# First feed-forward product of tiles 4 to 15 by one Strassen level, in blocks of 512 tokens

## The chip, the core and the metric

The kernel runs on one core of a Trainium2 chip. Its engines work side by side and meet at semaphores: TensorE (PE: matmuls out of SBUF into PSUM), VectorE (DVE), ScalarE (ACT), GpSimd (POOL) and SyncE (SP), and the DMA queues that SyncE and ScalarE feed. The metric is the device time of one launch in microseconds, lower is better. Before the change it is 388.39 us, the median of three runs (388.04 to 388.52).

## The reference

One transformer block on 2048 tokens of width 576, in bf16. Only its shape matters here:

```
h = layernorm(x) * (1 + ca) + sa
x = x + ga * attention(h)        # 32 heads of 18, linear attention, then @ wo
h = layernorm(x) * (1 + cb) + sb
x = x + gb * (relu(h @ w1) @ w2) # w1: 576 x 4608, w2: 4608 x 576
```

`attention` makes features phi(q), phi(k) of width 36 a head, sums kv over all tokens, and gives each token phi(q) kv / (phi(q) z).

## The kernel before

The 2048 tokens are 16 tiles of 128. A first part, whose order is written out word by word in `ORDER`, does the norms, the k, v and q projections of all tiles, the sums kv, the attention of tiles 0 and 1, and the loads of the weights. Its last feature tiles of q go to HBM (`eqd`) and come back later.

The second part is a loop over 8 blocks of 256 tokens (two tiles). A block has two stages, and its program order is the order of the Python calls: each engine runs its own instructions in that order.

- `l1` is the first feed-forward product. The hidden width is 36 chunks of 128, taken as 18 pairs (one of each half). The input width 576 is 4 chunks of 128 and one of 64. `l1_full` (L673) does the chunks of 128 with 256-column matmuls; `l1_rest` (L680) does the chunks of 64, two at a time in the upper and lower half of the rows. The work is in three groups of three PSUM pairs. `relu` (L687 to L689) takes the two halves of the hidden chunks and tokens out of PSUM as A11, A12, A22 and the difference U3; L711 makes the sum U2.
- `l2` is the second product, by one Strassen level: 7 products of 18 matmuls of 288 columns (L735) in place of 8. Its weight sums T1 to T4 are made once, in block 0, by `t_part`, and all weights stay in SBUF (R1, R2, RT). X, Y and Z are the three PSUM banks of its sums. `fin` (L718 to L722) scales a result, adds the residual row in `x_sb` and leaves it to a store.

Into both stages go "hooks" for the next block: `attend` (scores L389, reciprocal and scaling L396 and L397, a DMA transpose), the output projection (`wo_rest` L807 and `wo_full` L813), the residual add (L411) and statistics (L238), `norm2` (L420, a DMA transpose), the scale and shift of the norm (L851), and `q_next` (sums L282, reciprocal L341, GpSimd's L344 and L289, a DMA transpose L348, a reload L337). The scores and the projection share one PSUM pair, `pair(3)`.

## Time and profile before

The profiled execution has a span of 386.3 us, from the first to the last instruction; the median of the runs is 388.39.

| what | from the profile |
|---|---|
| TensorE, matmuls | 379.6 us busy, 98% of the span, 3705 matmuls |
| VectorE, ScalarE, GpSimd | 63%, 41%, 32% |
| granted TensorE clock | 1.000 |
| DMA | 43.18 MB, mean 112 GB/s |
| first 90 us | the part in `ORDER` |
| one block of 256 tokens (blocks 1 to 4) | 36.71 us, TensorE busy for all of it |
| last block | from 348.44 us to the end, 37.86 us |

A line of the page's groups reads: line, engine, operation, output<-inputs, shape (partitions x elements, type), count | busy us, mean ns of one | idle us just before, and what ended the idle time. The chain that ended last follows the work back from the last instruction; in order of time each line has its start, its length and what ran.

### The profile page before, as it was taken

What the parts mean: (1) busy time and instruction counts of PE and PEld (TensorE: products, weight loads), DVE (VectorE), ACT (ScalarE), POOL (GpSimd) and SP (SyncE); (2) the same over time, 40 slices, a digit from 0 to 9 for tenths busy, and PEclk for the clock granted to TensorE, in tenths of its full rate; (3) what the DMA queues carried; (4) which work ended last, traced back from release to release, by engine and by line L of the source; (5) the groups of instructions that cost most, each with busy time, mean ns of one, the idle gap of its engine ahead of it and who ended that gap; (6) DMA issues with size and microseconds to landing.
All of it is one profiled execution on the core that took longest, in us unless ns stands there. A gap on an engine that the chain in (4) does not pass through costs nothing.

```text
span 386.3 us, 8923 instructions
## 1 busy us (share of the span) xinstructions
PE 379.6 (98%) x3705; PEld 309.7 (80%) x3705; DVE 242.6 (63%) x470; ACT 156.7 (41%) x380; POOL 125.3 (32%) x195
## 2 busy tenths in 40 slices
PE   7999999999999999999999999999999999999995
PEld 4887778888887887788888888887888788778874
DVE  2898998784898666744764584567456735542333
ACT  2689997688540233034303420451054023302510
POOL 2088889830106400620160035004500540041023
PEclk9999999999999999999999999999999999999999
DMA  7995799798510524241233024212631221200001
GB/s 301 420 417 209 261 394 360 137 259 277 84 34 19 75 53 51 47 110 34 50 76 82 20 49 110 48 19 52 122 36 20 46 63 36 36 0 32 3 0 34
DMA packets 48940, 43.18 MB, mean 112 GB/s; under 512 B 39297, under 2 KB 41986, under 8 KB 48130
## 3 DMA queue, kind: packets, MB, share of 16 engines
q1 hardware_dynamic: 48610, 42.41, 39.4%
q8 instruction: 29, 0.48, 0.5%
q10 hardware_dynamic: 288, 0.19, 0.2%
q14 instruction: 13, 0.11, 0.1%
HBM read 27.38 MB, written 5.90 MB: 86 GB/s over the span
## 4 chain that ended last, share of the span: by engine, by line
PE 87%; DMA 4%; ACT 4%; DVE 3%; issue 1%; POOL 1%; SPq 0%; POOLq 0%; DVEq 0%
PE PS L673 33%; PE PS L735 31%; PE PS L272 9%; PE PS L680 5%; PE PS L813 4%; ACT RT L277 3%; DMA x_sb<-in_xk_dram 2%; PE PS L389 2%; DMA R<-in_wkT_dram 2%; PE PS L322 1%; DVE Rk L282 1%; PE PS L406 1%; DVE st L238 1%; ACT RT L511 0%; PE PS L807 0%
## 5 line engine op out<-in xcount | busy, mean ns | idle before, releaser
L673 PE MATMUL PS<-h,R 128*128 128x256 bf16 x1152 | 132.1, 273 | 0.0
L673 PEld LDWEIGHTS <-R 128*128 128x128 bf16 x1152 | 111.4, 98 | 14.1 <-issue 0.6
L735 PEld LDWEIGHTS <-RH 128*128 128x128 f16 x846 | 82.7, 98 | 20.7
L721 POOL TENSOR_TENSOR yt<-yt,gb_row 128x288 f32<-128x288 f32 x23 | 28.0, 1219 | 202.7 <-DVE yt L720 202.7
L687 ACT ACTIVATE RH<-PS 128x256 f16<-128x256 f32 x72 | 27.5, 382 | 110.6 <-PE PS L680 92.3
L735 PE MATMUL PS<-R,RH 128*128 128x288 bf16 (+1 forms) x558 | 72.1, 286 | 0.0
L689 DVE SCALAR_TENSOR_TENSOR RH<-PS,RH 128x256 f16<-128x256 f32 x72 | 28.6, 412 | 61.0 <-ACT RH L687 61.0
L688 ACT ACTIVATE RH<-PS 128x512 f16<-128x512 f32 x72 | 42.9, 596 | 5.5 <-PE PS L673 4.6
L277 ACT ACTIVATE RT<-PS,rs 128x576 bf16<-128x576 f32 x64 | 42.8, 742 | 2.3 <-PE PS L272 1.8
L735 PE MATMUL PS<-RT,RH 128*128 128x288 f16 x288 | 37.9, 286 | 0.0
L739 ACT ACTIVATE RS<-PS 128x288 f32<-128x288 f32 x24 | 9.8, 410 | 65.2 <-PE PS L735 65.2
L272 PE MATMUL PS<-RH,R 116*128 116x288 bf16 x240 | 32.5, 286 | 0.1
L272 PE MATMUL PS<-RH,RT 116*128 116x288 bf16 x240 | 31.9, 286 | 0.3
L720 DVE TENSOR_TENSOR yt<-PS,RS 128x288 f32<-128x288 f32 x23 | 10.5, 455 | 31.0 <-PE PS L735 21.9
L238 DVE BATCH_NORM_STATS2 st<-x_sb 128x6 f32<-128x288 bf16 x64 | 25.9, 447 | 4.0 <-DMA x_sb<-in_xk_dram 3.4
L272 PEld LDWEIGHTS <-RT 116*128 116x128 bf16 x240 | 22.9, 98 | 6.0 <-issue 0.5
L272 PEld LDWEIGHTS <-R 116*128 116x128 bf16 x240 | 22.7, 98 | 6.0 <-issue 0.5
L722 POOL TENSOR_TENSOR x_sb<-yt,x_sb 128x288 bf16<-128x288 f32 x31 | 22.7, 731 | 2.9 <-DVE yt L718 1.1
L282 DVE TENSOR_REDUCE Rk<-RT 128x64 f32<-128x1152 bf16 x16 | 21.3, 1336 | 0.9 <-ACT RT L277 0.7
L282 DVE TENSOR_REDUCE Rq<-RT 128x64 f32<-128x1152 bf16 x16 | 21.5, 1343 | 0.0
L680 PE MATMUL PS<-h,R 64*128 64x256 bf16 x288 | 19.9, 271 | 0.0
L411 DVE TENSOR_TENSOR x_sb<-x_sb,PS 128x576 bf16<-128x576 bf16 x16 | 12.1, 754 | 11.3 <-PE PS L813 10.2
(119 smaller groups left out, 418.8 us busy)
## 6 DMA issues: line engine op xcount, KB each, us to landing
R<-in_w1a_dram SPq DMA_DIRECT2D x4, 1152.0 KB, 8.2
eqd<-RT SPq DMA_DIRECT2D x12, 288.0 KB, 2.1
RT<-eqd SPq DMA_DIRECT2D x12, 288.0 KB, 3.5
R<-in_w2b_dram SPq DMA_DIRECT2D x2, 1296.0 KB, 8.1
R<-in_w2a_dram SPq DMA_DIRECT2D x3, 864.0 KB
out_dram<-x_sb SPq DMA_DIRECT2D x15, 144.0 KB, 2.1
RT<-in_xT_dram SPq DMA_DIRECT2D x2, 640.0 KB, 14.0
x_sb<-in_xk_dram SPq DMA_DIRECT2D x3, 288.0 KB
```

The costliest lines, as they stand in the source:

```text
L238: dve.bn_stats(out=s[:, hf, :], in_=x_sb[:, t, hf * HD:(hf + 1) * HD])
L272: pe.matmul(pr[:, k, 0:HD], lhsT=xt(t, ck), rhs=w[0:R, ck, k * HD:(k + 1) * HD], start=(ck == 0), stop=(ck == NC - 1))
L277: act.activation(out=E.rearrange("p (b h s e) -> p b h s e", b=2, s=2, e=DH)[:, :, :, s, :], in_=pr[:, :, 0:HD].rearrange("p b (h e) -> p ...
L282: dve.tensor_reduce(out=Rr, in_=E.rearrange("p (c e) -> p c e", e=DH), axis=AXX, op=ALU.add)
L673: pe.matmul(PS[:, 2 * u + hf, n * 256:n * 256 + 256], lhsT=w1a[:, ci, jj * P:(jj + 1) * P], rhs=hb[:, ci, :], start=(n == 0 and ci == 0), ...
L680: pe.matmul(PS[:, 2 * u + hf, n * 256:n * 256 + 256], lhsT=w1b[b0:b0 + 64, j * P:(j + 1) * P], rhs=hb[b0:b0 + 64, 4, :], start=False, stop ...
L687: act.activation(out=A11[:, j, :], in_=lo[:, :, 0, :], func=ACT.Relu)
L688: act.activation(out=A2[:, j, :, :], in_=PS[:, 2 * u + 1, :].rearrange("p (n s f) -> p n s f", n=2, s=2), func=ACT.Relu)
L689: dve.scalar_tensor_tensor(out=U3[:, j, :], in0=lo[:, :, 1, :], scalar=0.0, in1=A11[:, j, :], op0=ALU.max, op1=ALU.subtract)
L721: pool.tensor_tensor(out=y, in0=y, in1=gb_row[:, c], op=ALU.mult)
L722: pool.tensor_tensor(out=x_sb[:, t, c], in0=y, in1=x_sb[:, t, c], op=ALU.add)
L735: pe.matmul(PS[:, bank, 0:HD], lhsT=am[:, j, :], rhs=bm[:, j, :], start=first and j == 0, stop=(j % 9 == 8), skip_group_check=True)
```

## The change

Tiles 0 to 3 (two blocks of 256) go as before. Tiles 4 to 15 go in three blocks c of 512 tokens, with new stages.

- `c_l1` is the first product of 512 tokens by one Strassen level over tokens x input (the chunks of 128) x hidden. Each of 9 groups makes two pairs of hidden chunks by 7 products of 4 matmuls (L928), where 8 products of 4 stood. Four of the seven use sums of the weights, f16, three of them in three rotating slots (`ring`) in the upper half of `x_sb`, and one in place of w1 itself; four use sums of the activations, S1 to S4 (`h_sums`). Partial sums stay in PSUM: ScalarE copies a bank into another and one into SBUF (L959, L961), VectorE adds that to a bank, into PSUM (L981, L998), and further matmuls go on adding there. Four matmuls with zeros a block (`set_bits`) touch the upper columns of four banks. The chunks of 64 stay as they were, in one run a group (`ham`).
- The weight sums are made in blocks 0 and 1 by `sums1`, go to HBM (`w1td`, `sums1_out`), and come back piece by piece (`ring_in`). `x_sb` holds eight tiles then, and the rows of later tiles are loaded again.
- `c_l2` is the second product for 512 tokens: the same seven products, each for the two halves p of 256 columns. Its weights are seven quarters a block, read from HBM into four slots (`quarter_in`, ScalarE's queue); T1 to T4 are written to HBM once (`sums2_out`).
- The hooks of a block of 512 cover four tiles: the sums of q in `c_l1`, the scores, projection and norms in `c_l2`. Tiles 6 to 15 use the projection with ten full matmuls (`wo_mm`). The subtraction A12 - U2 goes from VectorE to GpSimd, in three parts.

```diff
--- before.py
+++ after.py
+NG = NK // 2
...
+    w2td = dram.tile([4, P, TW], FP16, name="w2td")
+    w1td = dram.tile([P, NG, 6 * 2 * P], FP16, name="w1td")
...
-    oT = small([P, 2, NC, P], BF16, "oT")
+    oT2 = [small([P, 2, NC, P], BF16, "oT"), carve(me, 0, (2, NC, P))]
+
+    def oT(t):
+        return oT2[t // 2 % 2][:, t % 2]
+
...
-    w2 = [carve(R2[i], 0, (NK, D)) for i in range(2)]
+    SLOTS = [R2[0][:, 0:TW], R2[1][:, 0:TW], R2[0][:, TW:], R2[1][:, TW:]]
+    B11, B21, B12, B22 = (v.rearrange("p (a b) -> p a b", b=HD) for v in SLOTS)
+    T3 = carve(R2[0].bitcast(FP16), TW, (NK, HD))
+    RTh = RT.bitcast(FP16)
+    T1, T4, T2 = (carve(RTh, i * TW, (NK, HD)) for i in range(3))
...
-        if b > 0:
-            dve.tensor_tensor(out=A12, in0=A12, in1=U2, op=ALU.subtract)
+        for k in range(3):
+            v, u = (x[:, 6 * k:6 * k + 6, :] for x in (A12, U2))
+            pool.tensor_tensor(out=v, in0=v, in1=u, op=ALU.subtract)
...
+    def attend(t, pr, double):
+        num_mm(t, pr)
+        num_o(t, pr)
+        if double:
+            act.activation(out=o_sb[:, t % 2, D:640], in_=o_sb[:, t % 2, 512:D], func=ACT.Copy)
+        turn_dma(oT(t), o_sb[:, t % 2, :])
...
+    ring = x_sb[:, 8:16, :].rearrange("p a b -> p (a b)").bitcast(FP16).rearrange(
+        "p (s m c f) -> p s m c f", s=3, m=3, c=2)
...
+    def sums1(k, s):
+        t1, t2, t4 = (ring[:, s, m] for m in range(3))
+        w12, w11, w22, w21 = (wq_slots(*i, k)[:, s] for i in ((0, 1), (0, 0), (1, 1), (1, 0)))
+        for o, p, q in ((t1, w12, w11), (t2, w22, t1), (t4, w21, t2)):
+            dve.tensor_tensor(out=o, in0=p, in1=q, op=ALU.subtract)
+
+
+    def sums1_out(k):
+        act.dma_start(w1td[:, 3 * k:3 * k + 3, :], ring.rearrange("p s m c f -> p s (m c f)"))
+
...
+    def ring_in(n):
+        g = n % NG
+        act.dma_start(ring[:, g % 3].rearrange("p m c f -> p (m c f)"), w1td[:, g, :])
+
+    QUART = (("in", 0), ("in", 2), ("t", 1), ("t", 0), ("t", 2), ("t", 3), ("in", 3))
+
+    def quarter(n):
+        kind, i = QUART[n % 7]
+        v = SLOTS[n % 4]
+        return (v if kind == "in" else v.bitcast(FP16)).rearrange("p (a b) -> p a b", b=HD)
...
+    def quarter_in(n):
+        kind, i = QUART[n % 7]
+        v = SLOTS[n % 4]
+        if kind == "in":
+            act.dma_start(v, w2in[:, i, :])
+        else:
+            act.dma_start(v.bitcast(FP16), w2td[i])
+
+    def sums2_out(i):
+        act.dma_start(w2td[i], flat((T1, T2, T3, T4)[i]))
...
+    def h_scale(k):
+        c = slice(2 * P * k, 2 * P * (k + 1))
+        for ci in range(NC):
+            act.activation(out=hc[:, ci, c], in_=hc[:, ci, c], func=ACT.Identity, scale=mod2[:, 1, ci:ci + 1],
+                           bias=mod2[:, 0, ci:ci + 1])
+
+    def h_sums():
+        a11, a12, a21, a22 = (hc[:, 2 * f:2 * f + 2, 2 * P * t:2 * P * (t + 1)] for t in range(2) for f in range(2))
+        for o, p, q, op in ((S1, a21, a22, ALU.add), (S2, S1, a11, ALU.subtract), (S3, a11, a21, ALU.subtract),
+                            (S4, a12, S2, ALU.subtract)):
+            dve.tensor_tensor(out=o, in0=p, in1=q, op=op)
+
+    def set_bits(bank):
+        pe.matmul(PS[:, bank, HD:512], lhsT=zero[:, 0:P], rhs=zero[:, 0:512 - HD], start=False, stop=True,
+                  skip_group_check=True)
+
+    def c_l1(c, mid, hooks, tail):
+
+        def xb(g):
+            return PS[:, 2 * (g % 2), :]
+
+        def yb(g):
+            return PS[:, 1 + 2 * (g % 2), :]
+
+        def zb(g):
+            return PS[:, 6 - 2 * (g % 2), :]
+        qb, rb = PS[:, 5, :], PS[:, 7, :]
...
+        def first(g):
+            mm(xb(g), raw(w1a, 0, 0, g), A11, g, True)
+            act.activation(out=yb(g), in_=xb(g), func=ACT.Copy)
+            mm(qb, tw(0, g), S1, g, True)
+            act.activation(out=dd[:, g % 2, :], in_=qb, func=ACT.Copy)
...
+        def group(g):
+            cur, prev, q = g < NG, g > 0, g - 1
+            if cur and prev:
+                first(g)
+            if prev:
+                act.activation(out=js(cA11, q), in_=yb(q), func=ACT.Relu)
+                mm(zb(q), raw(w1a, 1, 1, q), S4, q, False)
+                if not cur:
+                    tail(0)
+                mm(xb(q), tw(2, q), A22, q, False)
+            if g == 0:
+                set_bits(6)
+            if cur:
+                mm(xb(g), tw(1, g), S2, g, False)
+                dve.tensor_tensor(out=zb(g), in0=xb(g), in1=dd[:, g % 2, :], op=ALU.add)
+            top = (rest(yb(g), g, 0, True) if cur else []) + (rest(xb(q), q, 1, True) if prev else [])
+            low = (rest(zb(q), q, 0, False) + rest(rb, q, 1, False)) if prev else []
+            ham(top, low)
+            if prev:
+                dve.scalar_tensor_tensor(out=js(cU3, q), in0=xb(q), scalar=0.0, in1=js(cA11, q), op0=ALU.max,
+                                         op1=ALU.subtract)
+                act.activation(out=js(cA22, q), in_=rb, func=ACT.Relu)
+                act.activation(out=js(cA12, q), in_=zb(q), func=ACT.Relu)
+            if cur:
+                mm(yb(g), raw(w1a, 1, 0, g), A12, g, False)
+                if g == 0:
+                    set_bits(7)
+                mm(xb(g), raw(w1h, 0, 1, g), S3, g, False)
+                if g == 0:
+                    set_bits(3)
+                    set_bits(4)
+                dve.tensor_tensor(out=rb, in0=xb(g), in1=dd[:, g % 2, :], op=ALU.add)
+            mid(g)
+            if prev:
+                pool.tensor_tensor(out=js(cU2, q), in0=js(cU3, q), in1=js(cA22, q), op=ALU.add)
+                n = NG * c + q + 3
+                if n < NG * NCB:
+                    ring_in(n)
+            hooks(g)
...
+        def prod(i, p, lo, hi):
+            banks, am = ((XB, cA11), (YB, cA12), (XB, cU2), (ZB, cA11), (XB, cU3), (XB, cA22), (ZB, cA12))[i]
+            first = i in (0, 3)
+            bm = quarter(7 * c + i)
+            for j in range(lo, hi):
+                if j % 9 == 0:
+                    hooks(done[0])
+                    done[0] += 1
+                    if done[0] == 28 and ahead:
+                        ahead()
+                pe.matmul(PS[:, banks[p], 0:HD], lhsT=am[:, j, p * P:(p + 1) * P], rhs=bm[:, j, :],
+                          start=first and j == 0, stop=(j % 9 == 8), skip_group_check=True)
...
+        def body():
+            prod(0, 0, 9, NK)
+            for i in range(7):
+                for p in range(2):
...
+                        prod(i, p, 0, NK)
+                    ta, tb = t0 + p, t0 + 2 + p
+                    if i == 0:
+                        act.activation(out=PS[:, YB[p], 0:HD], in_=PS[:, XB[p], 0:HD], func=ACT.Copy)
+                    if i == 1:
+                        fin(ta, 0, YB[p], None)
+                        dve.tensor_tensor(out=cols(cA11, p), in0=cols(cU2, p), in1=cols(cA11, p), op=ALU.add)
+                        for k in range(3):
+                            v, u = (cols(x, p)[:, 6 * k:6 * k + 6, :] for x in (cA12, cU2))
+                            pool.tensor_tensor(out=v, in0=v, in1=u, op=ALU.subtract)
+                    if i == 2:
+                        copy(p, 1)
+                    if i == 4:
...
+                    if i == 5:
+                        fin(tb, 0, XB[p], None)
...
+                    if i == 6:
+                        fin(ta, 1, ZB[p], CS[p][1])
+                        store(ta)
+                    if p == 0 and i and 7 * c + i + 3 < 7 * NCB:
+                        quarter_in(7 * c + i + 3)
+            if not last:
+                quarter_in(7 * c + 10)
...
+            q_next(5)
+            sums2_out(1)
+        if pos == 9:
+            q_next(6)
+        if pos == 10:
+            sums2_out(2)
+        if pos == 11:
+            hb = h2[:, 1]
+            for ci in range(NC):
+                dve.tensor_scalar(out=hb[:, ci, :], in0=hb[:, ci, :], scalar1=mod2[:, 1, ci:ci + 1],
+                                  scalar2=mod2[:, 0, ci:ci + 1], op0=ALU.mult, op1=ALU.add)
+        if pos > 10:
+            sums1(2, pos - 11)
...
+        if g and u == 1:
+            pool.memset(o_sb[:, g - 1, D:640], 0.0)
+            attend(5 + g, LOW, False)
+        if (g, u) == (1, 1):
+            q_next(NT)
+        if (g, u) in ((1, 0), (1, 1), (1, 2)):
+            sums1(1, u)
+        if (g, u) == (2, 0):
+            sums1_out(1)
...
+    def b1_l2(pos):
+        if pos == 0:
+            norm2(4, quad(4))
+            norm2(5, quad(5))
+        if pos in (2, 5):
+            t = 6 + pos // 5
+            wo_mm(t, LOW)
+            residual(t, LOW)
+        if pos in (4, 7):
+            t = 6 + pos // 7
+            norm2(t, quad(t))
+        if pos in (1, 3, 4):
+            sums1(0, (1, 3, 4).index(pos))
+        if pos == 6:
+            sums1_out(0)
+        if pos == 8:
+            sums1_in_place(0)
+        if pos in (9, 11):
+            h_scale(pos // 11)
+        if pos == 12:
+            h_sums()
+            quarter_in(2)
...
+        def mid_l1(g):
+            if more and g in (2, 4, 6, 8):
+                q_tail(t + g // 2 - 1)
...
+        def in_l1(g):
+            if c == 0 and g in (0, 2):
+                sums1_in_place(1 + g // 2)
...
+            if g == 2:
+                s = t % 8
+                act.dma_start(x_sb[:, s:s + 4, :], a["xk"][:, t * D:(t + 4) * D].rearrange("p (t d) -> p t d", d=D))
+            if g in (1, 3, 5, 7):
+                q_head(t + g // 2)
...
+            i = {2: 0, 4: 1, 6: 2, 8: 3}.get(pos)
+            if i is not None:
+                attend(t + i, ATT, False)
+            i = {9: 0, 11: 1, 13: 2, 15: 3}.get(pos)
+            if i is not None:
+                wo_mm(t + i, ATT)
+                residual(t + i, ATT)
+            i = {11: 0, 13: 1, 15: 2, 17: 3}.get(pos)
+            if i is not None:
+                norm2(t + i, quad(t + i))
+            if pos in (19, 23):
+                h_scale(pos == 23)
+            if pos == 25:
+                h_sums()
...
+    l1(0, b0_l1)
+    l2(0, b0_l2)
+    l1(1, b1_l1)
+    l2(1, b1_l2, heads[0])
+    quarter_in(3)
+    for c in range(NCB):
+        tail, body = c_l2(c, l2s[c][1], heads[c + 1] if c + 1 < NCB else None)
+        tails = [tail]
+        bodies[c]()
+        body()
```

## The prediction

> **What bounds the kernel now.** I read the page's first part, then the chain that ended last (its shares, then in order of time), then the timeline around the matmul mode changes, then the groups by shape, and last the lines of GpSimd's products.
>
> The page: TensorE is busy nearly the whole span, and the chain is mostly TensorE, two thirds of it in the two feed-forward products (L673 and L735).
>
> ```profile
> PE 379.6 (98%) x3705; PEld 309.7 (80%) x3705; DVE 242.6 (63%) x470; ACT 156.7 (41%) x380; POOL 125.3 (32%) x195
> PE 87%; DMA 4%; ACT 4%; DVE 3%; issue 1%; POOL 1%; SPq 0%; POOLq 0%; DVEq 0%
> ```
>
> One pair of tiles on the chain (columns: start, length, what). All pieces are TensorE's and join up, so this stage has no wait to win; only fewer or shorter matmuls help. A 256-column matmul takes 5.24/48 = 0.1092 us, a 288-column one 15.43/126 = 0.1225.
>
> ```profile
> 201.59 3.06 PE PS L673 x28
> 204.64 0.76 PE PS L680 x12
> 205.40 0.48 PE PS L389 x10
> ...
> 211.50 0.76 PE PS L680 x12
> 212.38 1.09 PE PS L813 x8
> 213.47 5.24 PE PS L673 x48
> ...
> 222.87 15.43 PE PS L735 x126
> ```
>
> The timeline prices a change between full and half-row matmuls. The 48 full ones are issued from 139.88 to 145.12, and the half-row run starts at 145.22: 0.10 us lost. Its six pairs go out at about 0.109 (to 145.87), and the full ones after the last pair (0.122 from 145.88) start at 146.10: 0.10 again, so 0.19 a run with rounding. The last line gives a hand-over: eight matmuls end at 140.04 by the model (issue ends at 139.88), VectorE starts at 140.08, 0.20 after issue.
>
> ```profile
> 138.89 1.15 PE L813 MATMUL PS<-wo_sb,oT 128*128 128x288 bf16 x8
> 139.88 5.40 PE L673 MATMUL PS<-h,R 128*128 128x256 bf16 x48
> ...
> 145.22 0.83 PE L680 MATMUL PS<-h,R 64*128 64x256 bf16 x12
> ...
> 145.88 0.29 PE L807 MATMUL PS<-wo_sb,oT 64*128 64x288 bf16 x2
> 146.10 1.15 PE L813 MATMUL PS<-wo_sb,oT 128*128 128x288 bf16 x8
> ...
> 140.08 0.76 DVE L411 TENSOR_TENSOR x_sb<-x_sb,PS 128x576 bf16<-128x576 bf16 x1 [0.81 <-PE PS L813]
> ```
>
> Durations for the new work (mean ns after the comma):
>
> ```profile
> L688 ACT ACTIVATE RH<-PS 128x512 f16<-128x512 f32 x72 | 42.9, 596 | 5.5 <-PE PS L673 4.6
> L689 DVE SCALAR_TENSOR_TENSOR RH<-PS,RH 128x256 f16<-128x256 f32 x72 | 28.6, 412 | 61.0 <-ACT RH L687 61.0
> L743 DVE TENSOR_TENSOR RH<-RT,RH 128x2304 f16<-128x2304 f16 x8 | 10.9, 1358 | 3.8 <-PE PS L735 3.8
> L720 DVE TENSOR_TENSOR yt<-PS,RS 128x288 f32<-128x288 f32 x23 | 10.5, 455 | 31.0 <-PE PS L735 21.9 <-POOL x_sb L722 9.1
> ```
>
> GpSimd and VectorE get in each other's way: the same product takes 0.73 us or 4.68 (min/median/max), and VectorE's subtraction 1.05 or 1.90.
>
> ```profile
> L721 POOL TENSOR_TENSOR yt<-yt,gb_row x23: 728/730/4682, 119.1 to 378.5; 128x288 f32<-128x288 f32 x23
> L465 DVE TENSOR_TENSOR RT<-R,RT x6: 1048/1050/1900, 102.5 to 120.9; 128x1728 f16<-128x1728 bf16 x6
> ```
>
> **The change, part by part.** The sum is against the profiled execution, span 386.3; the median of 388.39 is 2.1 more, and I carry that over. A measurement tells about 0.2% (0.8 us) from no change.
>
> *TensorE's issue.* (a) Per 512 tokens the first product has 28 matmuls in each of 9 groups, 252, where 288 stood: 108 fewer in three blocks, 108 x 0.1092 = -11.8. (b) Half-row matmuls, equal in number, stood in 3 runs per 256 tokens, 6 per 512; now one per group and one after, 10. Four more runs at 0.19, and the first and last run each lack partners for two (one slot more each, 0.11): +0.98 a block, +2.9. (c) Four zero matmuls of 224 columns a block, 12 x 0.096: +1.15. (d) The output projection of tiles 6 to 15 is ten full matmuls (1.225) in place of a pair and eight (1.10): +1.2. The second product keeps its count, and f16 runs like bf16 in its rows (286 ns both). Sum: -6.5. All of it is on the path.
>
> *The group loop.* Per group TensorE issues 28 x 0.1092 + 4 x 0.109 + 0.19 = 3.69. ScalarE has five 512-wide passes at about 0.65 from start to start (0.60 and a gap): 3.25, hidden. VectorE has two adds into PSUM and one relu-subtract; no row writes PSUM, so from L720's 455 at 288 and a slope near 1.04 ns per element I take 0.69 each, 0.56 start to start. The tight chain: S2's matmuls end, 0.20, add, relu-subtract, next group's first matmul into the bank just read: 0.20 + 0.56 + 0.69 + 0.05 = 1.50. TensorE needs for the work between 0.63 + 2 x 0.437 = 1.50. No slack, so any excess is paid 27 times. I take 0.6 in all; bounds 0 and 0.2 a group (5).
>
> *Streaming.* A quarter of the second weights (1296 KB) is issued 2.5 products (11 us) ahead; the same size landed in 8.1 us before, amid other loads. The first product's sums come in 384 KB pieces with about 4.2 us from issue to use; 288 KB landed in 2.7 to 3.7. I take nothing: what hides them is those products and a group. If that cover is gone, see the third rival. ScalarE issues them in its own order, behind work already released, so nothing queues long.
>
> *Attention inside the second product (blocks of tiles 4 and 8).* Here I see a new wait. One PSUM pair serves the scores of four tiles and then the projection. After product 1's first half VectorE has the final multiply (0.46), the 2304-wide add (1.36), then reciprocal and scaling (0.35 + 0.76) of the third tile: done 3.0 us after that half. The fourth tile's scores are wanted at 0.39 + 18 x 0.1225 = 2.6: 0.4 lost. The second half repeats it: VectorE is done 2.8 later, while the projection is wanted 0.39 + 9 x 0.1225 = 1.5 after those scores start: 1.2 lost. That makes 1.6 a block as the floor. GpSimd now runs three 768-wide subtractions (about 1.48 each, an estimate from 1166 ns at 576 and 2322 at 1280), and if the second add waits behind one it adds 0.85 (1.90 less 1.05): ceiling 2.5. Of the adds beside GpSimd most keep their time (L465's median), some do not; I take 2.0, twice: +4.0. The first scores of each such block wait about 0.3 for two relus of the last group: +0.6.
>
> [...]
>
> *Tiles 0 to 3.* VectorE gets 27 subtractions of 512 for the first weights' sums (0.42 each, from 554 at 768; three in a chain 1.25). End of block 0: three chains and one more attention sum, while the subtraction that went to GpSimd (needed by the last product) competes with them: 0 to 2.5, I take 1.2. Block 1, first product: between the projection of tile 4 and the third relu stand 0.2 + 0.76 + 1.0 + 1.25 + 0.3 + 1.11 + 1.25 + 0.42 = 6.3 of VectorE, and TensorE wants that bank after 0.87 + 0.39 + 1.31 + 2.62 = 5.2: 1.1. Block 1, second product: VectorE starts 1.5 late with 10.7 before tile 7's second norm; logarithm, scaling, transpose (2.6 to 4.1), four passes of 0.49 and the sum follow: 18.2 to 19.7, wanted at 13 x 1.10 + 2.45 + 0.44 = 17.2: 1.0 to 2.5, I take 1.8. Together +4.1, bounds 0.5 and 7.
>
> *The end.* Half-width products, two short VectorE steps and a 2 us store, as before: 0.
>
> Sum: -6.5 + 0.6 + 4.0 + 0.6 + 4.1 = +2.8: span 389.1, time 391.2.
>
> **The rivals.**
> 1. *The saving stays (faster).* If VectorE's backlog in tiles 0 to 3 fits in TensorE's own slack and only the attention floor is paid, waits are 3.2 + 0.6, and the time is 388.4 - 6.5 + 3.8 = 385.7. For it: VectorE had 63% only, idle near 125 us. It decides when all waits stay under 6.5.
> 2. *VectorE bounds the group loop (slower).* If writing PSUM costs 0.1 us more per add than my 0.69, the chain grows by 0.1 to 0.2 in 27 groups, 2.7 to 5.4 on top: 394 to 397, at 0.25 it is 400. For it: no slack; against: the slopes of all PSUM readers agree.
> 3. *A 384 KB piece comes late.* At 3.7 plus a third it needs 4.9, 0.7 over; in the eight groups with attention transfers that is 5.6, in all 27 it is 19: 397 to 410. Against it: 2.7 when quiet, which gives 3.6.
> 4. *The matmuls are not fewer or not faster.* Only if mixed f16 and bf16 ran slower; both stand at 286 ns in L735. Nothing for it.
>
> [...]
>
> **How the numbers follow.** Forecast (waits 7.3 to 13, 389.2 to 395): 0.49. Rival 1: 0.23, all faster. Between them, within 0.2%: 0.05. Rival 2: 0.15. Rival 3: 0.07. Others, slower: 0.01. So faster 0.23, same 0.05, slower 0.72. The range takes rival 1 down to 384 and rivals 2 and 3 up to 400; the forecast's own is 389.2 to 395.
>
> **What would show it.** Right: 1044 full first-product matmuls, no idle between them beyond 0.1 us a group; gaps of 0.4 and over 1 us on TensorE at the fourth scores and first projection of two blocks, released by VectorE; a gap before the first S1 product. Wrong: group periods well over 3.7 us, gaps released by a DMA, or no gaps at those places.

## The result, and the profile after

The changed kernel takes 424.96 us (median of four runs, 423.2 to 425.4) against 388.22 for the kernel before: a ratio of 1.094, 95% interval 1.092 to 1.096. The profiled execution has a span of 423.4 us (before: 386.3). Slower was forecast; 36.7 us slower was not, the forecast was 391.2 and its range ended at 400.

The page of the changed kernel: TensorE's busy share, the clock that it was granted in 40 slices of the span, and the engines' shares of the chain that ended last.

```profile
PE 385.6 (91%) x3607; PEld 303.5 (72%) x3609; DVE 269.1 (64%) x483; ACT 193.5 (46%) x427; POOL 189.9 (45%) x242
...
PEclk9999999999999899999999996899989986999999
...
PE 63%; DVE 14%; DMA 13%; ACT 6%; issue 2%; SPq 1%; ACTq 0%; DVEq 0%
```

TensorE's share of the chain fell from 87% to 63%; VectorE (3% before) and the transfers (4% before) took its place. And around TensorE's long waits the granted clock falls, to 0.6 in one slice, which the page of before does not show.

In the line numbers of the changed kernel, L928 is the first product of tiles 4 to 15, L1025 their second product, L399 the scores, L416 the output projection, L411 the DMA transposes (`turn_dma`), L900 and L907 the scaling and the sums of the transposed rows (`h_scale`, `h_sums`), L867 the ring pieces, L880 and L882 the quarters, L751 the second product of tiles 0 to 3. The groups of instructions, costliest first (busy us, mean ns; then the idle time before them and what ended it):

```profile
L928 PE MATMUL PS<-RT,x_sb 128*128 128x256 f16 x216 | 34.1, 283 | 19.4 <-DVE RT L907 19.4
...
L981 DVE TENSOR_TENSOR PS<-PS,RT 128x512 f32<-128x512 f32 x27 | 18.9, 700 | 26.2 <-PE PS L928 26.1
L998 DVE TENSOR_TENSOR PS<-PS,RT 128x512 f32<-128x512 f32 x27 | 18.9, 700 | 8.3 <-PE PS L928 8.3
...
L900 ACT ACTIVATE h<-h,mod 128x256 bf16<-128x256 bf16 x30 | 15.4, 587 | 27.3 <-DMA h<-xn 27.2
...
L907 DVE TENSOR_TENSOR RT<-h 128x512 f16<-128x512 bf16 x6 | 2.5, 422 | 25.3 <-ACT h L900 25.3
```

Read the first and the last two lines backwards: TensorE's first S1 product of a block waited 19.4 us in all for VectorE's sums, VectorE for ScalarE's scaling, and ScalarE 27.2 us for a transfer, the transpose of the norm into h. The chain around the worst of these places, at the end of the block of tiles 4 to 7 (start, length, what):

```profile
244.13 0.42 ACT RS L1029
...
245.12 15.18 DMA h<-xn
...
261.39 1.08 ACT h L900 x2
...
262.49 0.44 DVE RT L907
...
262.97 1.01 PE PS L928 x4
263.98 2.16 PE PS L1025 x9
```

The last tile's transpose is issued at 245.12 and is on the chain for 15.18 us. A second such place, 334.05, lasts 14.05 us. In the kernel before, the transposes into h landed 2.6 us after issue:

```profile
DMA to landing us min/median/max: 2.6/2.6/2.6
```

The last two lines of the chain show the clock: nine 288-wide matmuls took 2.16 us, 0.24 each, twice the 0.1225 of the prediction's row. The stretches of that time give the same (columns: stretch, its length, busy time of PE, PEld, DVE, ACT, POOL, granted clock, DMA share, GB/s):

```profile
244.00:250.00 6.00, 6.00 (x51) 4.79 (x50) 1.69 (x5) 3.27 (x7) 3.30 (x5) 1.00 0.91 267
250.00:256.00 6.00, 4.45 (x37) 3.46 (x36) 0.46 (x1) 0.00 (x0) 1.04 (x2) 1.00 1.10 111
256.00:262.00 6.00, 0.00 (x0) 0.00 (x0) 0.00 (x0) 1.61 (x4) 0.00 (x0) 0.60 0.54 190
262.00:268.00 6.00, 5.03 (x24) 2.98 (x24) 3.05 (x7) 2.03 (x4) 2.59 (x4) 0.55 0.70 253
```

For six microseconds TensorE does nothing, and from 250 to 262 only 111 to 190 GB/s move although a quarter and a transpose are under way; 253 to 267 GB/s move in the stretches around.

What two transfers were doing there stands in the trace's packet records. The transpose goes out in packets of 256 bytes on SyncE's queue, a quarter in packets of 10368 bytes on ScalarE's. From 246.5 to 248.5 each queue started 17 to 21 packets per half microsecond: they take turns, one short packet for each long one of about 0.4 us. Alone, from 242.0 to 243.0, transposes ran at 330 to 430 packets per half microsecond. Here it is the short packets that pay for the turns.

That is the smaller part. Thirteen long packets which started at 249.9 to 250.4 took 2.5 to 8.7 us each instead of 0.4, and from 251 to 259.5 only 6 to 45 of the transposes' packets started in a microsecond: 9 of the 15.18 us. At the second place hardly any turns are seen before that (no transpose packet starts from 332 to 336, with a quarter under way); then twelve long packets from 337.2 to 337.7 took 2.5 to 6.1 us, and the transpose crawls until 346.4. Why the packets stood still is open.

TensorE's matmuls from start to start, less the interval at which they are issued, give this account of the span (us; the terms that the prediction had, beside what was found):

| term | predicted | found |
|---|---|---|
| TensorE's issue | -6.5 | -6.5 (by the run that closes the account, below) |
| group loop | +0.6 | +1.9 |
| streaming: S1 waits after tiles 4 to 7 and 8 to 11 | 0 | +17.6 |
| slow clock after waits | not in the sum | +8.2 |
| attention in the second product | +4.6 | +5.6 |
| tiles 0 to 3 (waits alone) | +4.1 | +10.6 |

-6.5 + 1.9 + 17.6 + 8.2 + 5.6 + 10.6 = 37.4, against 423.4 - 386.3 = 37.1.

### The profile page after: what moved, and what is told of

The parts are those of the page before. It is cut to its first block, busy times and chain, and to the rows that moved or that the text cites. A ratio compares the mean times of both kernels' runs of the same rounds, so it can differ in the third digit from the quotient of the medians.

```text
span 423.4 us, 9054 instructions
## 1 busy us (share of the span) xinstructions
PE 385.6 (91%) x3607; PEld 303.5 (72%) x3609; DVE 269.1 (64%) x483; ACT 193.5 (46%) x427; POOL 189.9 (45%) x242
## 4 chain that ended last, share of the span: by engine, by line
PE 63%; DVE 14%; DMA 13%; ACT 6%; issue 2%; SPq 1%; ACTq 0%; DVEq 0%
PE PS L928 21%; PE PS L1025 14%; PE PS L282 10%; DMA h<-xn 9%; PE PS L683 5%; PE PS L945 4%; ACT RT L287 3%; PE PS L416 3%; DVE x_sb L857 2%; DMA R<-in_wsh_dram 2%; DMA oT<-o_sb 2%; DVE RT L474 1%; DVE st L248 1%; ACT h L900 1%; PE PS L819 1%
## 5 line engine op out<-in xcount | busy, mean ns | idle before, releaser
L1025 PE MATMUL PS<-R,RT 128*128 128x288 bf16 (+1 forms) x414 | 56.2, 295 | 0.0
L928 PE MATMUL PS<-RT,x_sb 128*128 128x256 f16 x216 | 34.1, 283 | 19.4 <-DVE RT L907 19.4
L928 PEld LDWEIGHTS <-x_sb 128*128 128x128 f16 x324 | 32.3, 100 | 24.3 <-issue 19.9
L1025 PEld LDWEIGHTS <-RT 128*128 128x128 f16 x414 | 41.4, 101 | 11.5
L928 PEld LDWEIGHTS <-R 128*128 128x128 bf16 (+1 forms) x432 | 40.0, 98 | 12.4 <-issue 6.0
L1025 PE MATMUL PS<-R,RH 128*128 128x288 f16 (+1 forms) x324 | 42.2, 286 | 0.0
L1025 PEld LDWEIGHTS <-RH 128*128 128x128 f16 x324 | 31.3, 98 | 8.3 <-issue 0.6
L683 PE MATMUL PS<-h,R 128*128 128x256 bf16 x288 | 35.5, 281 | 1.2 <-DVE RH L699 0.8
L981 DVE TENSOR_TENSOR PS<-PS,RT 128x512 f32<-128x512 f32 x27 | 18.9, 700 | 26.2 <-PE PS L928 26.1
L928 PE MATMUL PS<-h,R 128*128 128x256 bf16 x216 | 33.0, 275 | 0.0
L683 PEld LDWEIGHTS <-R 128*128 128x128 bf16 x288 | 28.6, 101 | 5.8 <-issue 1.6
L1054 POOL TENSOR_TENSOR RT<-RT 128x768 f16<-128x768 f16 x18 | 32.3, 1819 | 0.0
L928 PE MATMUL PS<-RT,R 128*128 128x256 f16 x216 | 31.9, 273 | 0.0
L751 PEld LDWEIGHTS <-RH 128*128 128x128 f16 x216 | 21.1, 98 | 9.7 <-issue 4.5
```

Of the source, the lines that this page charges most:

```text
L683: pe.matmul(PS[:, 2 * u + hf, n * 256:n * 256 + 256], lhsT=w1a[:, ci, jj * P:(jj + 1) * P], rhs=hb[:, ci, :], start=(n == 0 and ci == 0), ...
L751: pe.matmul(PS[:, bank, 0:HD], lhsT=am[:, j, :], rhs=bm[:, j, :], start=first and j == 0, stop=(j % 9 == 8), skip_group_check=True)
L928: pe.matmul(o[:, n * 2 * P:(n + 1) * 2 * P], lhsT=w(ci, n), rhs=h[:, ci, :], start=(first and n == 0 and ci == 0), stop=False, skip_group_ ...
L981: dve.tensor_tensor(out=zb(g), in0=xb(g), in1=dd[:, g % 2, :], op=ALU.add)
L1025: pe.matmul(PS[:, banks[p], 0:HD], lhsT=am[:, j, p * P:(p + 1) * P], rhs=bm[:, j, :], start=first and j == 0, stop=(j % 9 == 8), skip_grou ...
L1054: pool.tensor_tensor(out=v, in0=v, in1=u, op=ALU.subtract)
```

## The experiments

The main theory: transposes are starved by the quarters beside them. The rival: the norm's chain over ScalarE and VectorE is late by itself. Each run stands beside the kernel before on the same chip (388.1 to 388.3).

**Transposes of the last two tiles on TensorE.**

```
             if i is not None:
-                norm2(t + i, quad(t + i))
-            if pos in (19, 23):
-                h_scale(pos == 23)
+                norm2(t + i, quad(t + i)) if i < 2 else norm2_pe(t + i)   # no transfer
+            if pos == 19:
+                h_scale(0)
+            if pos in (22, 24):
+                turn_pe(t + pos // 2 - 9, ATT)      # five transposes on TensorE
+                evict(t + pos // 2 - 9, ATT)        # scale and shift out of PSUM
```

> The quarters stay where they are; the third and fourth tile of each block in the second product are transposed by TensorE and scaled out of PSUM, so no transpose shares the DMA engines with the late quarters. Theory A: idle before S1 falls from 19.4 us to 4 to 7, time 403 to 410 (ten small TensorE transposes a block cost about 1 us). Rival B, the norm chain is itself late: idle over 14, time over 418.

Measured: 406.28 us. One line of its groups:

```profile
L949 PE MATMUL PS<-RT,x_sb 128*128 128x256 f16 x216 | 32.4, 273 | 2.1 <-DVE RT L928 2.1
```

The idle time before S1 fell from 19.4 to 2.1 us, which is the first block's alone, where no late quarter stood. The norm chain is in time once its transposes are off the DMA engines, though this edit also changes who does the scaling; the run without streaming, below, leaves that chain as it is and decides against the rival. The slow clock in tiles 4 to 15 fell from 6.6 to 3.2.

**Quarters held back.** The first form, in which a fifth quarter was moved as well (into group 9, over one still in use, so the products after it are not the reference's):

```
-                    if p == 0 and i and 7 * c + i + 3 < 7 * NCB:
+                    if p == 0 and 0 < i < 5 and 7 * c + i + 3 < 7 * NCB:
                         quarter_in(7 * c + i + 3)
-            if not last:
-                quarter_in(7 * c + 10)
...
         def in_l1(g):
+            if c and g >= NG - 3:
+                quarter_in(7 * c + 1 + g - (NG - 3))
```

> The three quarters that are issued while the last tiles' transposes run (the second, third and fourth after the one at product 4) are issued in the last three groups of the next first product instead. Theory A, transposes slowed by the quarters that share the DMA engines with them: the last transpose of a block lands in 2.6 to 6 us instead of 14 to 15, TensorE's idle time before the S1 product released by VectorE's sums falls from 19.4 us in all to 3 to 5 (2.3 of it in the first block, which has no such quarter and stays), the slow clock after it goes too (2.3 and 2.7 us), and the time falls from 425 to 402 to 408. Rival B, the norm chain on ScalarE and VectorE is itself too late: the idle stays over 14 us and the time over 418. Rival C, the quarters are then late for the second product: idle before the second product's matmuls released by a DMA appears, several us a block.

Measured: 443.64 us. It says little, since TensorE waited 34.3 us for quarters in the second product; the idle time before S1 is 2.2 us here too. The second form bounds g below NG:

```
+            if c and NG - 3 <= g < NG:
```

> As the first run that held the quarters back, but only the second, third and fourth quarter of the next second product are moved into groups 6, 7 and 8 of the next first product (the first run moved a fifth into group 9, which replaced a quarter still in use). Theory A, transposes slowed by those quarters: as with the transposes on TensorE, the idle time before S1 falls from 19.4 us to 3 to 5, and the time to 404 to 410. Rival C, the quarters then come late for the second product, or slow its first transposes: idle released by a DMA, over 1 us a block, and a time over 412.

Measured: 417.5, 420.5, 425.4 and 428.1 us; the profile is of the execution of 425.4. What theory A says of S1 and what rival C says of a new wait came true at once. Its groups:

```profile
L928 PE MATMUL PS<-RT,x_sb 128*128 128x256 f16 x216 | 32.9, 275 | 2.2 <-DVE RT L907 2.2
...
L399 PE MATMUL PS<-kvz,RE 128*128 128x76 bf16 (+2 forms) x160 | 9.2, 205 | 13.7 <-DMA RE<-RT 12.6 <-DVE yt L730 0.9 <-DVE o_sb L407 0.3
```

and its chain, at the end of the first product of tiles 8 to 11:

```profile
287.21 26.15 DMA RE<-RT
313.36 10.89 DMA oT<-o_sb
```

The S1 waits are gone (2.2), as theory A has it; but the quarters now stand beside the transposes of the attention's exponentials, and the next block's scores wait 12.6 us for those. Two transposes held SyncE's sequencer for over 9 us each while they were issued. Moving the quarters moved the late transposes with them, in the one execution that was profiled.

**The same bytes in short packets.**

```
+        for k in range(6):
+            w = slice(3 * HD * k, 3 * HD * (k + 1))
             if kind == "in":
-                act.dma_start(v, w2in[:, i, :])
+                act.dma_start(v[:, w], w2in[:, i, w])
...
```

> Each quarter goes out as six transfers of 216 KB at the same place, so its packets are a sixth as long (1728 bytes instead of 10368), with the same bytes at the same time. Theory A1, the two queues alternate packet by packet, so a transpose of 256-byte packets waits for one long packet per packet of its own: with short packets it lands in 4 to 7 us, TensorE's idle before S1 falls from 19.4 to 5 to 9, time 408 to 414. Rival A2, the bytes themselves or a stall of the DMA engines are what delays it: landing stays over 11 us and the idle over 14.

Measured: 425.98 us, no gain. The groups and a part of ScalarE's timeline tell why:

```profile
L930 PE MATMUL PS<-RT,x_sb 128*128 128x256 f16 x216 | 33.0, 276 | 12.1 <-ACT PS L961 8.1 <-DVE RT L909 3.9
```

```profile
247.11 3.34 ACTq L882 DMA_DIRECT2D R<-in_w_dram  x6
...
262.96 5.12 ACTq L884 DMA_DIRECT2D R<-w2td  x6
268.19 0.58 ACT L961 ACTIVATE PS<-PS 128x512 f32<-128x512 f32 x1 [5.05 <-DMA R<-w2td]
```

The wait for the transposes' sums fell from 19.4 to 3.9, so A1 was right on what it named, and no packet in this run took over 2.3 us. But six issues a quarter hold ScalarE's own queue for 3.34 and 5.12 us where a whole quarter's issue takes 0.33, and the copies behind them (L961) are late, 8.1 us. The second product waits 3.5 us more for ScalarE, and the projection 6.5 us where it waited 4.1. The time expected was missed, for waits that I had not put in.

**One queue for both.**

```
-            act.dma_start(v, w2in[:, i, :])
+            sp.dma_start(v, w2in[:, i, :])
         else:
-            act.dma_start(v.bitcast(FP16), w2td[i])
+            sp.dma_start(v.bitcast(FP16), w2td[i])
```

> One word changed: the quarters are issued on SyncE's queue, where the transposes are, in the same place of the program; same packets, same bytes. Theory A2, two loaded queues are what slows a transpose (its 256-byte packets take turns with 10368-byte ones); in one queue a transpose only waits until the quarter ahead of it is through: the idle before S1 falls from 19.4 us to 4 to 10, time 408 to 417. Rival K, a transpose near a quarter is late in any order: idle over 14 us, time over 418.

Measured: 410.09 us. Groups, and one piece of the chain:

```profile
L928 PE MATMUL PS<-RT,x_sb 128*128 128x256 f16 x216 | 33.4, 279 | 8.4 <-DMA x_sb<-w1td 6.2 <-DVE RT L907 2.2
```

```profile
261.76 8.00 DMA x_sb<-w1td
```

Same packets, same bytes, same places in the program, and the S1 waits of the late blocks are gone, with no packet over 2.3 us. Two loaded queues make the starvation, as A2 of this run's expectation has it (not the A2 of the run with short packets). What differs as well is the time of the quarters, for SyncE's order puts each behind the transposes ahead of it: they go out at 241.77, 246.66 and 251.31 where ScalarE sent them at 236.18, 244.13 and 246.40. But being close to a quarter is not enough to starve: the two last transposes of the block, issued at 243.95 and 245.24, stood right behind a quarter of this queue, and their last packets had started by 249.4. A new wait of 6.2 us comes in: the first ring piece of the next two blocks, still on ScalarE's queue, takes 8 us beside the last quarters, on SyncE's. That is the prediction's third rival, in a kernel that it was not made for.

**No streaming.**

```
-                    if p == 0 and i and 7 * c + i + 3 < 7 * NCB:
+                    if p == 0 and i and 7 * c + i + 3 < 7 * NCB and False:
...
-            if not last:
-                quarter_in(7 * c + 10)
```

> The changed kernel with the streaming of the second weights left out: no quarter is loaded while tiles 4 to 15 are computed, so their second product works on stale weights; nothing else is changed, the transposes stay DMA transposes. This prices the step that the prediction took at 0. Theory A': all transposes of tiles 4 to 11 are slowed by the quarters, those of the attention output too: the last two S1 waits (17.6 us) fall under 1.5 in all, the projection's waits (4.4) to 1.5 to 3 in all (what VectorE's order leaves), the slow clock from 8.2 to 2 to 4; time 425 less 22 to 28, so 397 to 403. Rival B, the norm chain itself is late: S1 waits over 6 us remain, time over 406.

Measured: 400.98 us, 24.0 under the changed kernel. Its groups:

```profile
L928 PE MATMUL PS<-RT,x_sb 128*128 128x256 f16 x216 | 32.4, 273 | 2.2 <-DVE RT L907 2.2
...
L416 PE MATMUL PS<-wo_sb,oT 128*128 128x288 bf16 x60 | 8.3, 286 | 3.5 <-DVE o_sb L407 3.5
```

So the step that the prediction took at nothing costs 24 us: 17.6 of S1 waits, 6.6 of slow clock and 0.6 of the projection's waits come to 24.8. The norm's chain is untouched here and in time: the rival falls. In this run the attention's waits are VectorE's alone: 0.45 at the fourth scores and 1.92 at the first projection, per block.

**VectorE's order in the attention.** Two runs with one edit, with quarters and without. The base of the first is the kernel with transposes on TensorE, that of the second the one without streaming.

```
                     if i == 1:
-                        fin(ta, 0, YB[p], None)
-                        dve.tensor_tensor(out=cols(cA11, p), in0=cols(cU2, p), in1=cols(cA11, p), op=ALU.add)
+                        def add(p=p):
+                            dve.tensor_tensor(out=cols(cA11, p), in0=cols(cU2, p), in1=cols(cA11, p), op=ALU.add)
...
+                        elif p == 0:
+                            later[6] = [add]
+                            later[8] = [lambda ta=ta: fin(ta, 0, YB[0], None)]
+                        else:
+                            later[8].append(add)
+                            later[9] = [lambda ta=ta: fin(ta, 0, YB[1], None)]
```

What stands in `later` runs after the hook of that position: the attention of the third tile is at 6, of the fourth at 8, the first projection at 9.

> With the same base (406.3 us), VectorE's multiply and 2304-wide add after product 1 of tiles 4 to 11 are put behind the scaling of the third and fourth attention tile instead of ahead of it. Theory H, those two instructions are what makes the fourth scores (0.45 us, twice) and the first projection (2.4 to 2.6, twice) wait: both go below 0.5 in all, and the slow clock after them (3.2 us) goes too; time 397 to 400. Rival I, the transpose of the attention output or the single PSUM pair is late by itself: at most 2 us of change, 404 to 406.

> The run without streaming, with VectorE's multiply and add after product 1 also put behind the scaling of the third and fourth attention tile. Theory H', what is left of the attention waits once no quarter is under way is VectorE's order, as the prediction had it (1.6 to 2.5 us a block): 2 to 5 us faster than the run without streaming. Rival I', it is the transposes alone: within 1 us of it.

With quarters 407.98 us against 406.28: no gain, as rival I has it, though above its 404 to 406. The waits of the profiled execution are 0.5 us less than in its base, and the clock costs 3.5 us more, at two places that the edit does not touch (128.4 and 179.6 us). Without quarters 398.84 against 400.98: 2.1 less, theory H', and as much between two executions at full clock (398.22 and 400.29). A stretch of the first run's timeline:

```profile
222.32 1.28 SPq L411 DMA_TRANSPOSE oT<-o_sb  x1
...
226.31 0.36 DVE L406 RECIPROCAL rden<-PS 128x32 f32<-128x32 f32 x1
229.23 0.76 DVE L407 TENSOR_TENSOR o_sb<-PS,rden 128x576 bf16<-128x576 f32 x1 [2.57 <-DMA oT<-o_sb]
...
230.04 1.35 PE L416 MATMUL PS<-wo_sb,oT 128*128 128x288 bf16 x8 [2.67 <-DVE o_sb L407]
```

The fourth tile's scaling has VectorE to itself and still waits 2.57 us, for the second tile's transpose to have read the buffer it writes. So two causes lay on top of each other at this place, and taking one away showed the other. Without quarters the deferral removes VectorE's part whole, and half of it comes back as a wait at the second projection:

```profile
L416 PE MATMUL PS<-wo_sb,oT 128*128 128x288 bf16 x60 | 8.3, 286 | 0.3
L416 PE MATMUL PS<-wo_sb,me 128*128 128x288 bf16 x60 | 8.3, 286 | 2.3 <-DVE x_sb L421 2.3
```

**Tiles 0 to 3.** Two prices on the base with transposes on TensorE (406.28). GpSimd's subtraction back on VectorE:

```
-        for k in range(3):
-            v, u = (x[:, 6 * k:6 * k + 6, :] for x in (A12, U2))
-            pool.tensor_tensor(out=v, in0=v, in1=u, op=ALU.subtract)
+        dve.tensor_tensor(out=A12, in0=A12, in1=U2, op=ALU.subtract)
```

> Beside the two transposes a block on TensorE (406.3 us, the base here), the subtraction A12 - U2 of tiles 0 to 3 goes from GpSimd (three of 2.44 us in tiles 0 and 1) back to VectorE (one of 1.36). Theory F, GpSimd's subtractions and VectorE's sums of T4 hold each other up: VectorE's three T4 sums take 1.0 us each instead of 1.0, 2.5 and 2.5, the two waits in the second product of tiles 0 and 1 (1.4 and 1.2 us) go, and the time falls by 2 to 4 to 402.5 to 404.5. Rival G, VectorE has simply too much to do there: its 1.36 us of extra work leaves the waits, time 405.5 to 408.

Measured: 404.11 us (403.1 and 405.1; the base 406.0 and 406.6), inside theory F's numbers. But the two waits did not go: the one for T4 fell from 1.41 to 0.82, that for the multiply stayed at 1.23, and the rest of the gain came later, as smaller waits at the scores (1.93 to 1.38) and before S1. VectorE's T4 sums in the base took 1.00, 2.49 and 2.49 us while GpSimd's three subtractions took 2.44 to 2.47 each; now they take 1.00, 1.10 and 2.02, so the last is still held up.

Most of the first weights' sums left out:

```
-        for o, p, q in ((t1, w12, w11), (t2, w22, t1), (t4, w21, t2)):
+        for o, p, q in ((t1, w12, w11),) if s == 0 else ():
```

> With the same base (406.3 us), 24 of the 27 subtractions that make the first weights' sums in tiles 0 to 3 are left out (about 10 us of VectorE), so the sums are not what the product needs. Theory G, VectorE's load in tiles 0 to 3 makes the waits there: those at the first scores of tiles 2 and 3 (1.9 us), the ones before the third relu (1.0) and before the first S1 product (2.3) go; time 401 to 403.5. Rival F, only GpSimd's subtraction does: under 1 us of change, 405.3 to 406.5.

Measured: 400.35 us (398.8 and 401.9), 5.9 less and a little under theory G's 401 to 403.5. The waits at the first scores of tiles 2 and 3 (1.93), before the third relu (0.98) and for the copy in the second product (1.79) are gone, the one before S1 is halved (2.31 to 1.08).

**The clock.**

```
+            if g == 0:
+                spin(80 if c else 20, 5, 256)
             mm(qb, tw(0, g), S1, g, True)
```

> Nothing is taken away; ahead of the first S1 product TensorE runs matmuls of zeros (20 in the first block, 80 in the other two, 2.2 and 8.7 us, about the length of the waits). Theory D, the slow clock after a wait comes from TensorE being idle: the matmuls behind the wait run at 109 ns from the start, 2.2 to 2.7 us less in the second and third block, time 418 to 422. Rival E, the clock falls for another reason (what runs at that time): the 213 ns stretch stays and the time is 424 to 427.

Measured: 425.13 us. The stretch that was idle, and the one after it:

```profile
256.00:262.00 6.00, 6.00 (x58) 5.37 (x55) 0.00 (x0) 0.00 (x0) 0.00 (x0) 1.00 1.04 149
262.00:268.00 6.00, 3.65 (x25) 2.67 (x23) 1.89 (x5) 3.64 (x7) 1.01 (x2) 0.85 0.76 269
```

The granted clock is 1.00 and 0.85 where it was 0.60 and 0.55; the run's mean is 0.992 instead of 0.968, and in tiles 4 to 15 the slow matmuls cost 3.3 us instead of 6.6. What remains follows the 2.5 us of wait left behind the spins at the first of the two places, and one of the projection's waits, where nothing spun. So idling is what costs the clock (theory D). The time missed its expectation because the spins and the 2.5 us of wait still left behind them came to 22.2 us where the waits had been 19.9, and the projection's waits grew by 0.6.

**The account closed.** Streaming left out, 24 of the 27 sums left out, the subtraction on VectorE:

```
+                    if p == 0 and i and 7 * c + i + 3 < 7 * NCB and False:
...
+        for o, p, q in ((t1, w12, w11),) if s == 0 else ():
...
+        dve.tensor_tensor(out=A12, in0=A12, in1=U2, op=ALU.subtract)
```

> The run without streaming, with 24 of the 27 sums of the first weights left out and A12 - U2 of tiles 0 to 3 on VectorE as well, so three of the prediction's cost steps are taken out and the arithmetic of TensorE stays. If the steps add up (6 us for the sums and 2.2 us for the subtraction, as measured beside the transposes on TensorE), it is 8 us under the run without streaming: 389 to 394. If TensorE's saving of 6.5 us is as computed, what is left over 381.9 us (388.4 less 6.5) must be found again as waits of the attention (2 to 5), of the groups (1.9), before S1 (1 to 2) and of the slow clock (1 to 3).

Measured: 392.56 us (span 390.8). The waits of this run:

```profile
L926 PE MATMUL PS<-RT,x_sb 128*128 128x256 f16 x216 | 32.4, 273 | 0.5 <-DVE RT L905 0.5
...
L751 PE MATMUL PS<-RT,RH 128*128 128x288 f16 x72 | 9.6, 286 | 0.7 <-DVE RT L474 0.7
...
L416 PE MATMUL PS<-wo_sb,oT 128*128 128x288 bf16 x60 | 8.3, 286 | 3.5 <-DVE o_sb L407 3.5
```

From start to start all its waits come to 11.06 us: attention 5.0, groups 1.9, the end of tiles 0 and 1 2.05, before S1 0.7, and five smaller ones 1.4. 386.3 - 6.5 + 11.06 = 390.9, and the span is 390.8. TensorE's saving is there to a tenth, and nothing unnamed is left.

**All the work, with the cures.** On the kernel with one queue, the last two quarters moved to group 6 of the next first product, with the deferral and the subtraction on VectorE:

```
+            if c and g == 6:
+                quarter_in(7 * c + 2)
+                quarter_in(7 * c + 3)
```

> All work is done. Quarters on SyncE's queue (410.1 us before), the last two of a block issued in group 6 of the next first product, A12 - U2 of tiles 0 to 3 on VectorE, and VectorE's multiply and add behind the attention's scaling. If the prices add up: less 6.1 (ring pieces late behind the last quarters), less 3.4 (the slow clock after that wait), less 2.1 and 2.0 to 2.2 for the two cures: 396.3 to 396.5, taken as 394 to 399. If a quarter makes transposes or ring pieces late wherever it stands: over 402, with an idle time released by a DMA.

Measured: 403.67 us (402.0 to 407.1): not what the prices add up to, but the expectation's other case, over 402 with an idle time released by a DMA.

```profile
L926 PE MATMUL PS<-RT,x_sb 128*128 128x256 f16 x216 | 32.9, 275 | 5.2 <-DMA x_sb<-w1td 3.5 <-DVE RT L905 1.7
```

Ring pieces are still late (3.5 us), and the scores and the first projection of tiles 8 to 11 wait 2.5 and 1.0, in the stretch into which the quarters were moved. The prices do not add up: a quarter that is moved away from one small transfer meets another. That the second wait is the quarters' doing is argued from its place; no run took it apart.

Then the sums, moved to where VectorE was idle in the run that closes the account:

```
+        if (g, u) == (0, -1):          # tiles 0 and 1, ahead of the first relu
+            for k in range(3):
+                sums1(2, k)
...
+        if (g, u) == (0, -1):          # tiles 2 and 3; the third of sums1(1) at (1, -1)
+            sums1(1, 0)
+            sums1(1, 1)
...
+        if pos == 8:                   # their second product; the first of sums1(0) is ahead of it
+            sums1(0, 1)
+            sums1(0, 2)
```

> The run before it in this set with the 27 sums moved: nine to the 4 us in which VectorE is idle before the first relu of tiles 0 and 1, nine to its idle time early in tiles 2 and 3, nine behind the last norm of tiles 4 to 7. If it is their place and not their 11 us that costs, most of the 5.9 us found when they were left out comes back: 390 to 394. Not under 388.3, the time before, for the run with streaming and sums left out still took 392.6, and the new order of the attention is worth 2.1 on top of that. If VectorE's total load costs, whatever the place: 395 to 399.

Measured: 406.34 us (403.1 to 407.7), no gain, and above both cases of the expectation. The waits named in the run without sums went or shrank, and others took their place (2.6 us at tiles 2 and 3's scores, for the residual of the tile before; 1.5 for an attention transpose in tiles 0 and 1). That speaks for VectorE's 11 us in those tiles as the cost, more than where they stand; no run shows it by itself. No version with all the work came near 388.2.

## Why the prediction was wrong

**The step that failed** is "*Streaming* ... I take nothing". It asked whether a quarter and a ring piece come in time, and they do: in the changed kernel no S1 wait and no second product waits for one. It never asked what a quarter does to the transfers beside it. For the transposes it carried prices from the kernel before, where they landed in 2.6 to 4.1 us and no quarter streamed in the same stretch. On the chain they cost 14 to 15 us. The runs with the transposes on TensorE, with one queue and without quarters show it three ways; the step's price is 24 us, two thirds of the whole loss. How the quarters do it is known in part: the queues take turns (17 to 21 packets of each in half a microsecond), but more than half of those 14 to 15 us are packets that stand still (9 of the 15.18), and why is open.

**A term missing** is the slow clock: 8.2 us, most of it (6.6) in tiles 4 to 15. Every wait in the sum was counted at its own length; a long one costs a slow stretch on top (2.3 us behind the wait of 8.5, 2.7 behind that of 8.7). The other 1.6 follow a wait of 1.93 us that cost no clock in several other runs.

**Tiles 0 to 3** were the right mechanism at less than half the size: 10.6 of waits and 1.6 of slow clock against 4.1. The end of block 0: 2.6 against 1.2. The first product of block 1: 3.9 against 1.1, where VectorE, late from T4, held up the first scores for 1.9 through the bank pair, which the step did not look at. The second product and S1: 4.1 against 1.8, of which 1.8 is ScalarE's copy behind the norm's scalings. The sums are 5.9 of it and the place of the subtraction 2.2.

**Right**: TensorE's issue, -6.5, by the run that closes the account, with 1044 full matmuls. **Attention**: 2.0 a block taken, floor 1.6, ceiling 2.5; without streaming the trace shows 0.45 + 1.92 = 2.4, at the two instructions named and released by VectorE. GpSimd beside the second add is visible too: 1.35 us for the first and 2.05 for the second, in both blocks of the changed kernel, so both second adds were held up. GpSimd's 768-wide subtractions take 1.82 on average where 1.48 was estimated. **Group loop**: 1.9 against 0.6 and inside its bounds; the add into PSUM takes 700 ns where 0.69 us was taken from slopes, the period is 3.79 against 3.69.

**The rivals**: the saving did not stay; the groups cost 1.9 us in all, not the 2.7 to 5.4 on top of the 0.6 that rival 2 has; a ring piece was late only in experiments. (In rival 2, 0.25 us in 27 groups is 6.75, which gives 398 and not 400.) None had a transpose as the late transfer. The list of signs did name "gaps released by a DMA" as what would prove the prediction wrong, though the page puts these under VectorE and ScalarE: they are found only by following the releasers back.

## What to carry to other kernels

Before adding a bulk stream, list the small transfers on the path that will run beside it, and price them for company: a landing time from a quiet stretch is no price (2.6 us here, and 14.05 to 15.18 on the chain beside quarters). One queue for the transposes and the bulk loads, or TensorE for the last two transposes of a block, took the wait for the S1 sums from 19.4 us to 2.2 and 2.1, though with one queue a ring piece then came 6.2 late. Moving the bulk in time only picked another victim (12.6 at the scores), and cutting it into pieces held up the engine that issued them (3.34 and 5.12 for six, 0.33 for one). The saving of 6.5 us in matmuls, 2%, is less than one of the waits of 8.5 and 8.7, and these also cost 2.3 and 2.7 of slow clock afterwards.

## What the runs showed that was not expected

- A DMA transpose beside quarters on another queue was on the chain for 14.05 to 15.18 us (2.6 alone; 5.9 and 7.7 for two others beside a quarter), and in one run held its sequencer for over 9 us. Packets of 10368 bytes that take 0.4 us took up to 9.5, and ring packets of 3072 up to 5.2, in the four runs where whole quarters on ScalarE's queue met a late transpose on SyncE's (the changed kernel, the spin and both held-back forms). No packet of 10368 bytes took over 2.3 us with one queue, with short packets, without quarters, or with the late transposes on TensorE. What stops them is not settled.
- Whether a wait costs the clock depended on where it fell. In all sixteen traces the granted clock changes only at whole multiples of 3.41 us from each other, from a start that differs from run to run; in that of the changed kernel it is 0.5 from 137.73 to 141.14 us, 257.19 to 267.43, 315.22 to 318.63 and 345.94 to 356.18 (1, 3, 1 and 3 times 3.41), and 1.0 between. Cut a trace from 95 us on into these stretches: there are 31 at full clock in which TensorE stood idle for 63% or more (gaps over 0.15 us between matmuls), and every one was followed by a stretch at half clock (213 or 240 ns a matmul instead of 109 or 122). Of the 1356 with less idling four were, at 56 to 57%. So the wait of 2.32 us before the first block's S1 cost the clock in two runs of ten, and one of 2.92 us that lay across two stretches did not.
- Two causes of the same wait hide each other: deferring VectorE's work gained nothing with the quarters there and 2.1 us without them.
